# A two-layer product with nested sums: where the second layer's odd transfers land, and which engine makes four sums of W_out

## The chip, the cores and the metric

The kernel runs on one core of a Trainium2 chip. The metric is device time in microseconds (us) of one execution. The engines of the core are named as in the profile: PE (TensorE, matrix products), DVE (VectorE), ACT (ScalarE), POOL (GpSimd) and SP (SyncE, which here only issues DMAs). A line number such as L901 is a line of the kernel before.

## The reference

A masked attention on four batches of eight heads gives `x`, 3072 rows of 512 values. The change does not touch it. What follows is a feed-forward block:

```python
h = x @ w_in                                  # 3072x512 by 512x2048
g = h * (1.0 / (1.0 + np.exp(-1.702 * h)))
return (g @ w_out).astype(np.float32)         # 3072x2048 by 2048x512
```

All numbers are float32.

## The kernel before, in words

**Products by sums.** Both layers are computed with Winograd's form of Strassen's scheme: a product of 2x2 blocks takes seven products instead of eight, numbered 1 to 7 in the code, and needs four sums of quarters of each operand. `sums_a` (L219) makes those of the left operand (W): `s1 = a21 + a22`, `s3 = a11 - a21`, `s2 = s1 - a11`, `s4 = a12 - s2`. `sums_b` (L227) makes those of the right operand: `t1 = b12 - b11`, `d12 = b22 - b12`, `t2 = b22 - t1`, `t4 = b21 - t2`. In the profile a sum has the line of its formula: L222 to L225 for W, L230 to L233 for the other side. Products of the second layer are nested twice, so there are outer sums of W_out, inner sums of those, and inner sums of `g`.

**First layer.** 24 steps n = 8·sb + mt (`sb` is a block of 1024 rows, `mt` a strip of 128 hidden columns). The last two, 22 and 23, run outside the nested pairs, in the loop at L1391, each through `hidden` (L1083). Step 23 issues its products in the order 6, 5, 7, 2, 4, 3 (its product 1 belongs to step 22). Product 5 goes to PSUM bank `b`. At L1109 DVE adds that bank to `c22`. Product 3 (L1127) is accumulated onto the same bank `b`, so PE may start it only when the sum of L1109 has read the bank; the trace has this sum, and all sums of this helper, under L919. Products 5 and 6 read the sums of W_in, `s_in[:, 0:2]`. The results of a step are put to `g_dram` as seven blocks: three straight from `hidden`, four as POOL sums in `outer_sums` (L1140), which runs for step 22 before `hidden` of step 23 is emitted, and for step 23 at its end.

**Second layer.** 21 steps n (three blocks of rows, outer products in the order 1, 2, 6, 7, 5, 3, 4). In `product_of_halves` (L1228) each has seven products of 128x256 tiles, in PE's order 1, 2, 3, 6, 7, 5, 4, one after another without a gap if all operands are there. The block of `g` of step n comes by `fetch(n)` (L1186), two DMAs of 1 MB on SP's queue (one of 2 MB for the last step): even n into columns of `w_in_sb` (rows of 2 KB, four to a partition and DMA), odd n into `raw_g` (8 KB in one piece). DVE makes the inner sums of `g` (`g_sums`, L1206): product 5 needs t1 (L230), product 6 needs t2 (L232), product 7 needs d12 (L231, in place), product 4 needs t4 (L233). Those of step n+1 are made during step n, at the places called `after(0)` to `after(3)`. DVE also adds up the products (L1244).

**W_out.** Its outer sums are made in halves `c`, `low` and `high` (L1341), each a list of four sums s1, s3, s2, s4 of 128x1024 values: in `high`, DVE makes s1 and s2 (`high[0]`, `high[2]`), POOL makes s3 and s4 (`high[1]`, `high[3]`). The inner sums of W_out (`inner_sums(at)`, L1176) are POOL's, each of 128x512 values, kept in `rooms` (L1163), pieces of `xT`, of `w_in_sb` columns that are no longer needed, and of `s_in`. Outer product at = 2 of the order (n = 2) uses `inner_sums(2)`, and so on.

**Order.** The order on PE, DVE, ACT and POOL is that of the program text (`manual_schedule`); each engine runs its own list in order and waits where an operand is missing. SP's DMAs stand in one queue too. What L1391 to L1414 emits around step 23 is therefore the order of DVE: `high[0]`, t1 of n = 0 (`g[0]`), then in step 23 the sums to `c22` and `u`, t2 (`g[1]`, emitted "between"), the sum to `v`, then `high[2]`, d12 and t4. POOL's order there is: the inner sums of n = 1, the four outer sums of step 22, the four of step 23, `inner_sums(2)`, `high[1]`, `high[3]`.

Of the kernel before, what the change touches and what calls it, by code (L numbers as in the profile page):

```python
# [19 lines left out]
P = 128  # L20
# [18 lines left out]
def kernel(  # L39
# [806 lines left out]
    def feed_forward(tag, late=()):  # L846
# [9 lines left out]
        with ExitStack() as fctx:  # L856
# [283 lines left out]
            def outer_sums(*args):  # L1140
                last = args[0] * MT + args[1] == n1 * MT - 1
                t = [x.tile([P, XT], F32, tag=f"t{i}", name=f"t{i}") for x in places_of_sums for i in (1, 2, 4)]
                if last:
                    t = [s_in[:, 2, i // 2, i % 2 * XT : (i % 2 + 1) * XT] for i in range(3)]
                for i, (f, kept) in enumerate(g_outer(*args, *(t or (args[2], args[5], args[4])))):
                    f()

                    if last and i > 1:
                        kept_late.append(kept)
                    else:  # L1150
                        kept()

            places_of_sums, kept_late = [], []

            wqs = []

# [2 lines left out]
            flat = s_in.rearrange("p i k f -> p (i k f)")  # L1159
            rooms, s_rooms = ([x[:, i * F4 * P : (i + 1) * F4 * P].rearrange("p (c d) -> p c d", d=P) for i in range(count)]  # L1160
                              for x, count in ((xT[:, 3], 4), (flat, 12)))
            in_rooms = [w_in_sb[:, :, F2 * i + mt * P : F2 * i + (mt + 1) * P] for mt in range(4, FC // 2) for i in range(2)]
            rooms += in_rooms[:4] + s_rooms[:8] + in_rooms[4:] + s_rooms[8:]  # L1163
            wholes = [xT[:, i, 4 * XT : 6 * XT] for i in range(4)] + [t_x[:, i].rearrange("p k t -> p (k t)") for i in range(2)]
            wholes = [x.rearrange("p (q t) -> p q t", q=4) for x in wholes]

# [14 lines left out]
                return sums_a(nc.gpsimd, *w_quarters(OUTER[at])) if at < len(OUTER) else []  # L1181

            steps_out = [(sb, o) for sb in range(n1) for o in OUTER]
            raw_g = [w_in_sb.rearrange("p c (i f) -> p (c i) f", i=2)[:, :, 0:XT], None]

            def fetch(n):  # L1186
                sb, o = steps_out[n]
                parts = 1 if n + 1 == len(steps_out) else 2
                for h in range(parts):
                    cs = slice(h * FC // 2 // parts, (h + 1) * FC // 2 // parts)  # L1190
                    yield loader[0].dma_start(out=raw_g[n % 2][:, cs], in_=g_dram[len(LEFT) * sb + RIGHT[o], :, cs, :])

            g_tiles, wide = {}, []

            def g_quarters(n):
                if n not in g_tiles:


                    g_tiles[n] = wholes[4:6] if n == 1 else [
                        st2.tile([P, F4, TH], F32, tag=t, name=t + "b") for t in ("t1", "t2")] if n % 2 else wide[0:2]  # L1200
                    g_tiles[n] = g_tiles[n] + [wide[2]]
                g = raw_g[n % 2]
                x = [g[:, F4 * k : F4 * (k + 1), TH * j : TH * (j + 1)] for k in range(2) for j in range(2)]
                return x + g_tiles[n]

# [132 lines left out]
            for i in (list(range(1, LATE + 1)) if late else []) + free[:FC]:  # L1338
                todo[i] = [lambda: next(steps)] * 6

            low, high = ([sums_a(eng, *(x[:, :, F4 * c : F4 * (c + 1), :] for x in wqs))[i] for i, eng in enumerate(engs)]  # L1341
                         for c, engs in enumerate(((nc.gpsimd, nc.vector, nc.gpsimd, nc.gpsimd),
                                                   (nc.vector, nc.gpsimd, nc.vector, nc.gpsimd))))
            first = 2 * NESTED.stop
            todo[first] = high[:1] + inner_sums(1)

# [44 lines left out]
            for n in range(2 * NESTED.stop, 3 * MT):  # L1391
                sb, mt = divmod(n, MT)
                between, end = [], []
                if n == 2 * NESTED.stop:
                    whole(fetch(0))
                else:
                    assert not agenda
                    inner_ctx.close()
                    nest_ctx.close()
                    cv_ctx.close()  # L1400
                    sets[:] = [fctx.enter_context(tc.tile_pool(name=f"f{2 + i}{tag}", bufs=1, space=PSUM, side=side))
                               for i, side in enumerate(("right", "left"))]
                    gp = fctx.enter_context(tc.tile_pool(name=f"gp{tag}", bufs=1))
                    raw_g[1] = gp.tile([P, FC // 2, XT], F32, name="raw_g")
                    whole(fetch(1))
                    wide += [stage.tile([P, 4, TH], F32, tag=x, name="wide") for x in ("u", "v", "c21", "c22")]
                    t_ctx = fctx.enter_context(ExitStack())
                    places_of_sums.append(t_ctx.enter_context(tc.tile_pool(name=f"ts{tag}", bufs=1)))
                    g = g_sums(0)
                    g[0]()  # L1410
                    outer_sums(*heads.pop("sums"))
                    between, end = g[1:2], high[2:3] + g[2:] + inner_sums(2) + [high[1], high[3]]
                hidden(sb, mt, between, todo.pop(n, []) + end)
                yield  # L1414
            t_ctx.close()
# [5 lines left out]
            for n, (sb, o) in enumerate(steps_out):  # L1421
                final = n + 1 == len(steps_out)
                if 0 < n and n + 1 < len(steps_out):
                    dmas = list(fetch(n + 1))
                    while kept_late:
                        kept_late.pop(0)()
                        for dma in dmas:
                            behind_issue(stored[-1], dma)

                if n in (2, 3, 5, 6):  # L1430

                    nc.gpsimd.tensor_copy(mark, (g_quarters(n)[5] if n < 4 else ms[OUTER[n - 1]])[0:1, 0, 0:1])
                for f in {2: inner_sums(3), 3: inner_sums(4), 5: inner_sums(5) + inner_sums(6)[:2], 6: inner_sums(6)[2:]}.get(n, []):
                    f()
                later_sums = g_sums(n + 1)
                m = wholes[n % len(wholes)]

                def after(at, last=None):
                    if at == 0:
                        while pending:  # L1440
                            pending.pop(0)()
                    todo = [[x] for x in later_sums] if n == 0 else [[], later_sums[0:1], later_sums[1:3], later_sums[3:]]
                    todo = todo[at] if not final else []
                    if n + 2 >= len(steps_out):
                        turns = [lambda q=q: turned(m, int(final), int(not final), q, q + 1, last if q == 2 else None) for q in range(4)]
                        write = [lambda x=(sb, int(not final), (h,), loader + [nc.scalar] * (final or h == 0)): written(*x) for h in range(2)]
                        if final:
                            todo = [[], last_sum, [turns[1]], [turns[3], write[1]], [turns[0]], [turns[2], write[0]]][at]
                        elif at == 2:
                            todo = [later_sums[1], turns[1], turns[3], write[1]]  # L1450
                        elif at == 3:
                            todo = [turns[2], turns[0], later_sums[2]]
                            pending.append(write[0])
                            last_sum.append(later_sums[3])
                    for f in todo:
                        f()

                acc = {6: 1, 7: 6, 2: 1, 3: 6, 4: 7}.get(o)
                if o == 3:
                    pending.pop(0)()  # L1460
                ms[o] = product_of_halves(n, None if acc is None else ms[acc], after)

                def flat(x):
                    return x.rearrange("p q t -> p (q t)")

                if o == 5:
                    m5, m6, m7 = (ms[i] for i in (5, 6, 7))
                    pending += [lambda a=m6, b=m5: nc.vector.tensor_tensor(flat(a), flat(a), flat(b), op=Alu.add),
                                lambda a=m5, b=m7: nc.vector.tensor_tensor(flat(a), flat(a), flat(b), op=Alu.add),
                                lambda a=m5: turned(a, 1, 1, 0, 4)]  # L1470
                elif o in (2, 3) and n + 2 < len(steps_out):
                    pending.append(lambda a=ms[o], j=int(o == 3): turned(a, 0, j, 0, 4))
                    if o == 3:
                        pending.append(lambda sb=sb: written(sb, 1, (0, 1), loader))
                elif o == 4 and not final:
                    pending.append(lambda a=ms[4]: turned(a, 1, 0, 0, 4))
                    pending.append(lambda sb=sb: written(sb, 0, (0, 1), loader))
                yield

    def whole(steps):  # L1480
        for _ in steps:
            pass
# [49 lines left out]
```

## Time and profile before

| | us |
|---|---|
| median of 3 runs | 851.23 |
| lowest and highest | 850.65, 851.99 |
| the profiled execution | 850.31 |
| its span (first to last instruction) | 848.5 |
| PE busy | 837.3 |
| DVE busy | 679.2 |
| POOL busy | 376.9 |
| ACT busy | 337.6 |

The profiled execution's time lies 1.81 us above its span, and 0.92 us below the median of the runs. A row of a timeline has the start, the duration, the engine, the line, the operation, what it writes and reads, the shape, the count of merged instructions, and in brackets the idle time before it with what ended it. A duration counts from when the engine takes up the instruction, so an instruction that is held up shows as a long one.

### The profile page before, as it was taken

The numbers are of one execution on the slowest core, as the hardware profiler recorded it, in microseconds if no ns is written. First come the engines' busy times: TensorE is split into PE (matmuls) and PEld (weight loads), VectorE is DVE, ScalarE is ACT, GpSimd is POOL, SyncE is SP. The second block draws the span as 40 slices with busy tenths as digits, with TensorE's granted clock in tenths as the row PEclk, the third lists the DMA queues.
The fourth block names the chain that finished last, engine by engine and source line by source line (L and its number), as shares of the span: only waits on it lengthen the run. The fifth ranks groups of instructions, "written<-read, shape, count | busy, mean of one in ns | idle before, by whom it ended". The sixth has DMA issues, their size and how long they took to land.

```text
span 848.5 us, 14972 instructions
## 1 busy us (share of the span) xinstructions
PE 837.3 (99%) x5662; PEld 523.2 (62%) x5662; DVE 679.2 (80%) x1079; ACT 337.6 (40%) x550; POOL 376.9 (44%) x322
## 2 busy tenths in 40 slices
PE   9999999999999999999999999999999999999996
PEld 4444444444444444565666666656888888888885
DVE  5478888887888985778887888847899977797776
ACT  7766766767675634433444344442000000000000
POOL 5433443434343359996843487858865100000000
PEclk9999999999999999999999999999999999999999
DMA  8688667677663104455555545667844685468524
GB/s 145 120 156 170 156 131 146 144 150 151 151 154 95 48 2 173 149 173 213 211 203 195 197 181 216 237 232 249 298 153 168 198 270 193 157 202 248 195 102 101
DMA packets 173149, 144.92 MB, mean 171 GB/s; under 512 B 124112, under 2 KB 140112, under 8 KB 170512
## 3 DMA queue, kind: packets, MB, share of 16 engines
q1 hardware_dynamic: 162160, 110.54, 46.8%
q10 hardware_dynamic: 10912, 33.39, 11.9%
q8 instruction: 45, 0.74, 0.4%
q14 instruction: 32, 0.26, 0.1%
HBM read 79.69 MB, written 50.33 MB: 153 GB/s over the span
## 4 chain that ended last, share of the span: by engine, by line
PE 97%; DVE 2%; POOL 1%; issue 0%; POOLq 0%
PE product L1239 29%; PE product L901 22%; PE s L547 15%; PE s L514 15%; PE small L971 7%; PE product L971 4%; PE s L496 2%; PE s L460 1%; PE s L569 1%; DVE xT L1244 1%; DVE wide L232 0%; POOL above L339 0%; PE s L410 0%; POOL feat L337 0%; DVE wide L1244 0%
## 5 line engine op out<-in xcount | busy, mean ns | idle before, releaser
L484 ACT ACTIVATE e<-s 128x768 f32<-128x768 f32 x192 | 143.2, 811 | 48.8 <-PE s L514 43.9
L547 PE MATMUL s<-e,v 128*32 128x385 f32 x1536 | 130.9, 488 | 0.0
L525 POOL TENSOR_TENSOR t_x<-e 128x768 f32<-128x768 f32 x32 | 60.6, 1892 | 136.2 <-ACT e L484 131.3
L901 PE MATMUL product<-xT,w_in_sb 128*128 128x512 f32 x208 | 96.8, 592 | 0.0
L547 PEld LDWEIGHTS s<-e,v 128*32 128x32 f32 x1536 | 46.7, 109 | 79.3 <-issue 62.6
L901 PE MATMUL product<-t_x,s_in 128*128 128x512 f32 x192 | 89.8, 592 | 0.0
L514 PE MATMUL s<-s_in 32*128 32x384 f32 x912 | 87.8, 481 | 0.0
L525 POOL TENSOR_TENSOR t_x<-t_x,e 128x768 f32<-128x768 f32 x32 | 55.2, 1724 | 43.4 <-ACT e L484 42.0
L538 DVE TENSOR_TENSOR acc<-acc,e 128x768 f32<-128x768 f32 x63 | 70.1, 1112 | 2.3
L1275 ACT COPY wide<-product 128x256 f32<-128x256 f32 x20 | 7.4, 372 | 161.2 <-PE product L1239 127.9
L901 PEld LDWEIGHTS product<-xT,w_in_sb 128*128 128x128 f32 x208 | 39.4, 190 | 31.8 <-issue 28.9
L514 PEld LDWEIGHTS s<-s_in 32*128 32x128 f32 x912 | 43.9, 185 | 23.4 <-issue 2.2
L901 PEld LDWEIGHTS product<-t_x,s_in 128*128 128x128 f32 x192 | 36.4, 190 | 28.1 <-issue 24.9
L919 DVE TENSOR_TENSOR u<-product,u 128x256 f32<-128x256 f32 (+1 forms) x64 | 29.7, 477 | 18.9 <-PE product L971 16.6
L514 PE MATMUL s<-own 32*128 32x384 f32 x432 | 44.3, 482 | 0.0
L465 DVE TENSOR_SCALAR f<-s,above,weight 128x384 bf16<-128x384 f32 x15 | 10.2, 677 | 39.3 <-PE s L569 33.9
L230 POOL TENSOR_TENSOR u<-v,u 128x1024 f32<-128x1024 f32 (+1 forms) x12 | 26.2, 2184 | 20.9 <-ACT v L916 12.4
L1239 PE MATMUL product<-w_in_sb,xT 128*128 128x256 f32 x152 | 35.1, 379 | 0.0
L535 DVE SCALAR_TENSOR_TENSOR acc<-t_x,e 128x768 f32<-128x768 f32 x31 | 29.3, 946 | 6.4 <-POOL t_x L525 3.5
L919 DVE TENSOR_TENSOR c<-small,c 128x256 f32<-128x256 f32 (+1 forms) x60 | 26.8, 461 | 9.2 <-PE small L971 9.1
L919 DVE TENSOR_TENSOR v<-small,v 128x256 f32<-128x256 f32 (+1 forms) x60 | 27.0, 464 | 7.3 <-PE small L971 4.9
L1035 ACT COPY c<-product 128x512 f32<-128x512 f32 x20 | 11.7, 587 | 52.0 <-DVE v L919 50.1
(299 smaller groups left out, 1807.2 us busy)
## 6 DMA issues: line engine op xcount, KB each, us to landing
w_in_sb<-g_dram SPq DMA_DIRECT2D x20, 1024.0 KB, 5.6
raw_g<-g_dram SPq DMA_DIRECT2D x20, 1024.0 KB, 6.1
g_dram<-c ACTq DMA_DIRECT2D x20, 512.0 KB, 3.0
raw<-in_moe_w_out_dram ACTq DMA_DIRECT2D x16, 512.0 KB, 3.7
raw<-in_moe_w_in_dram ACTq DMA_DIRECT2D x15, 512.0 KB, 3.8
s_in<-own SPq DMA_DIRECT2D x36, 192.0 KB, 4.0
v<-in_v_dram SPq DMA_DIRECT2D x16, 384.0 KB, 4.2
g_dram<-u ACTq DMA_DIRECT2D x10, 512.0 KB, 2.9
```

Of the source, the lines that this page charges most:

```text
L230: return [lambda: eng.tensor_tensor(t1, b12, b11, op=Alu.subtract), lambda: eng.tensor_tensor(b12, b22, b12, op=Alu.subtract), lambda: eng ...
L484: nc.scalar.activation(es[c][:, kt, :, 0:HS], ps[:, :, 0:HS], Act.Exp, scale=1.0 / D**0.5)
L496: nc.tensor.matmul(ps[:, j, 0:HS], a[hs, keys], m[hs, cols], start=at == 0, stop=at == 1)
L514: nc.tensor.matmul(ps[i][:, j, 0:HS], a[r0 : r0 + 32, keys], m[r0 : r0 + 32, cols], start=at == 0, stop=at == 2)
L525: nc.gpsimd.tensor_tensor(low_sum, low_sum if i else e[:, 0], e[:, i + 1], op=Alu.add)
L535: nc.vector.scalar_tensor_tensor(acc, terms[0], T * TINY, terms[1], op0=Alu.add, op1=Alu.add)
L538: nc.vector.tensor_tensor(acc, acc, terms[i + 1], op=Alu.add)
L547: nc.tensor.matmul(av[D * j + d : D * j + d + 32, :], vt[:, j, row, d : d + 32], es[c][:, t, j, :], start=(t == 0), stop=(t == T - 1))
L901: nc.tensor.matmul(ps, wq[LEFT[i]][:, kc, :], xq[RIGHT[i]][:, kc, :], start=(start and kc == 0), stop=(kc == K2 - 1), skip_group_check=not ...
L919: nc.vector.tensor_tensor(dst, x, y, op=Alu.add)
L971: nc.tensor.matmul(x, wq[LEFT[i]], xq[RIGHT[i]], start=start, stop=True, skip_group_check=True)
L1239: nc.tensor.matmul(ps, wq[LEFT[i]][:, c, :], gq[RIGHT[i]][:, c, :], start=(onto is None and c == 0), stop=(c == F4 - 1), skip_group_check= ...
```

## The change

Five things are done:

1. `raw_g` gets a third place. `fetch(0)` still lands in `w_in_sb`; odd n still land in the pool tile; even n from 2 on (the third transfer, the fifth, and so on) land in the first 4096 values per partition of `s_in`, in one piece per partition.
2. `fetch(2)` is issued in the middle of step 23 (`between`), not at the head of step 1 of the second layer; the stores of the last two outer sums of step 23 are no longer put behind it (`kept_late` is gone).
3. `rooms` are laid out anew, so that the inner sums stay clear of `s_in[:, 0:2]`: sixteen pieces of `w_in_sb` columns and the last four of `s_in`.
4. `high[1]` and `high[3]` are made by DVE instead of POOL.
5. DVE's order around step 23 is now: `high[0]`, t1, **t2, `high[2]`**, then the sums to `c22` and `u`, **`high[1]`**, the sum to `v`, **`high[3]`**, d12, t4. POOL's list loses the two sums at its end; the rest of its order is as before.

```diff
-                for i, (f, kept) in enumerate(g_outer(*args, *(t or (args[2], args[5], args[4])))):
-                    f()
-
-                    if last and i > 1:
-                        kept_late.append(kept)
-                    else:
-                        kept()
+                for f in g_outer(*args, *(t or (args[2], args[5], args[4]))):
+                    for x in f:
+                        x()
...
-            in_rooms = [w_in_sb[:, :, F2 * i + mt * P : F2 * i + (mt + 1) * P] for mt in range(4, FC // 2) for i in range(2)]
-            rooms += in_rooms[:4] + s_rooms[:8] + in_rooms[4:] + s_rooms[8:]
+            in_rooms = [w_in_sb[:, :, F2 * i + mt * P : F2 * i + (mt + 1) * P] for mt in (4, 5, 6, 0, 1, 2, 3, 7) for i in range(2)]
+            rooms += in_rooms + s_rooms[8:]
...
-            raw_g = [w_in_sb.rearrange("p c (i f) -> p (c i) f", i=2)[:, :, 0:XT], None]
+            raw_g = [flat[:, 0 : 4 * F2].rearrange("p (c t) -> p c t", t=XT), None,
+                     w_in_sb.rearrange("p c (i f) -> p (c i) f", i=2)[:, :, 0:XT]]
+
+            def raw_of(n):
+                return raw_g[n % 2 if n else 2]
...
-                         for c, engs in enumerate(((nc.gpsimd, nc.vector, nc.gpsimd, nc.gpsimd),
-                                                   (nc.vector, nc.gpsimd, nc.vector, nc.gpsimd))))
+                         for c, engs in enumerate(((nc.gpsimd, nc.vector, nc.gpsimd, nc.gpsimd), (nc.vector,) * 4)))
...
                     g = g_sums(0)
-                    g[0]()
+                    for f in g[:2] + high[2:3]:
+                        f()
                     outer_sums(*heads.pop("sums"))
-                    between, end = g[1:2], high[2:3] + g[2:] + inner_sums(2) + [high[1], high[3]]
+                    between, end = [lambda: fetch(2), high[1]], high[3:] + g[2:] + inner_sums(2)
                 hidden(sb, mt, between, todo.pop(n, []) + end)
...
                 if 0 < n and n + 1 < len(steps_out):
-                    dmas = list(fetch(n + 1))
-                    while kept_late:
-                        kept_late.pop(0)()
-                        for dma in dmas:
-                            behind_issue(stored[-1], dma)
+                    if n > 1:
+                        fetch(n + 1)
```

More of the change, by code (lines that the diff above doesn't have):

```diff
@@ L1144, in outer_sums @@
                     t = [s_in[:, 2, i // 2, i % 2 * XT : (i % 2 + 1) * XT] for i in range(3)]
-                for i, (f, kept) in enumerate(g_outer(*args, *(t or (args[2], args[5], args[4])))):
-                    f()
-                    if last and i > 1:
-                        kept_late.append(kept)
-                    else:
-                        kept()
-            places_of_sums, kept_late = [], []
+                for f in g_outer(*args, *(t or (args[2], args[5], args[4]))):
+                    for x in f:
+                        x()
+            places_of_sums = []
             wqs = []
@@ L1190, in fetch @@
                     cs = slice(h * FC // 2 // parts, (h + 1) * FC // 2 // parts)
-                    yield loader[0].dma_start(out=raw_g[n % 2][:, cs], in_=g_dram[len(LEFT) * sb + RIGHT[o], :, cs, :])
+                    loader[0].dma_start(out=raw_of(n)[:, cs], in_=g_dram[len(LEFT) * sb + RIGHT[o], :, cs, :])
             g_tiles, wide = {}, []
@@ L1201, in g_quarters @@
                     g_tiles[n] = g_tiles[n] + [wide[2]]
-                g = raw_g[n % 2]
+                g = raw_of(n)
                 x = [g[:, F4 * k : F4 * (k + 1), TH * j : TH * (j + 1)] for k in range(2) for j in range(2)]
@@ L1394, in feed_forward @@
                 if n == 2 * NESTED.stop:
-                    whole(fetch(0))
+                    fetch(0)
                 else:
@@ L1404, in feed_forward @@
                     raw_g[1] = gp.tile([P, FC // 2, XT], F32, name="raw_g")
-                    whole(fetch(1))
+                    fetch(1)
                     wide += [stage.tile([P, 4, TH], F32, tag=x, name="wide") for x in ("u", "v", "c21", "c22")]
```

## The prediction

> **What bounds the kernel now.** I read the page's chain first, then PE's waits from 560 us on, where the change works.
>
> ```profile
> PE 97%; DVE 2%; POOL 1%; issue 0%; POOLq 0%
> PE product L1239 <- DVE wide L232: 2.5, 2, 2.2
> ```
>
> PE is the chain: 97% of it. So an edit counts only by what PE waits. From 560 us to the end it waits for one thing, twice, 2.5 us together: t2 of a second-layer step (DVE, L232). No wait of PE for a DMA is listed there. Timeline rows of PE (two products of step 0, three of step 2, where the longer wait is), then of DVE and POOL ahead of that wait:
>
> ```profile
> 591.60 1.89 PE L1239 MATMUL product<-w_in_sb,xT 128*128 128x256 f32 x8
> 595.05 1.89 PE L1239 MATMUL product<-wide,w_out_sb 128*128 128x256 f32 x8
> 612.32 1.89 PE L1239 MATMUL product<-w_in_sb,s_in 128*128 128x256 f32 x8
> 616.40 1.97 PE L1239 MATMUL product<-wide,s_in 128*128 128x256 f32 x8 [2.19 <-DVE wide L232]
> 618.20 1.89 PE L1239 MATMUL product<-w_in_sb,xT 128*128 128x256 f32 x8
> ...
> 606.86 3.98 DVE L1244 TENSOR_TENSOR xT<-xT 128x256 f32<-128x256 f32 x2
> 610.75 2.57 DVE L1244 TENSOR_TENSOR xT<-xT,wide 128x256 f32<-128x256 f32 x1
> 613.25 1.21 DVE L230 TENSOR_TENSOR wide<-w_in_sb 128x1024 f32<-128x1024 f32 x1
> 614.38 0.74 DVE L1244 TENSOR_TENSOR xT<-product,xT 128x256 f32<-128x256 f32 x2
> 615.05 1.21 DVE L232 TENSOR_TENSOR wide<-w_in_sb,wide 128x1024 f32<-128x1024 f32 x1
> ...
> 606.73 1.33 POOL L225 TENSOR_TENSOR s_in<-xT,s_in 128x512 f32<-128x512 f32 x1
> 608.02 2.53 POOL L223 TENSOR_TENSOR w_out_sb<-w_out_sb 128x1024 f32<-128x1024 f32 x1
> 610.51 2.54 POOL L225 TENSOR_TENSOR xT<-w_out_sb,xT 128x1024 f32<-128x1024 f32 x1
> ```
>
> Products start 1.73 us apart (products 7 and 4 of step 0, with one between them: 595.05 - 591.60 = 3.45), so product 6 of step 2 was due at 612.32 + 1.73 = 614.05. It starts at 616.40, 2.35 late, 0.14 after t2 ends (615.05 + 1.21 = 616.26); the next one follows after 1.80 instead of 1.73. Cost: **2.42**. Why DVE is late: three adds of 128x256, two of them in the row of 3.98 us, end just after POOL's sums do (610.84 after 610.55, 613.32 after 613.05). Those two POOL sums are `high[1]` and `high[3]`.
>
> **How the two engines take turns.** The rows of step 23, in order of time:
>
> ```profile
> 570.81 2.35 POOL L232 TENSOR_TENSOR c<-c,u 128x1024 f32<-128x1024 f32 x1
> 575.10 1.22 DVE L222 TENSOR_TENSOR xT<-w_out_sb 128x1024 f32<-128x1024 f32 x1
> 576.23 1.22 DVE L230 TENSOR_TENSOR wide<-w_in_sb 128x1024 f32<-128x1024 f32 x1
> 576.61 3.05 POOL L233 TENSOR_TENSOR s_in<-c,c 128x1024 f32<-128x1024 f32 x1 [3.44 <-ACT c L916]
> 579.61 1.27 POOL L222 TENSOR_TENSOR w_in_sb<-w_out_sb 128x512 f32<-128x512 f32 x1
> 580.36 0.69 DVE L919 TENSOR_TENSOR c<-product,c 128x512 f32<-128x512 f32 x1 [2.91 <-ACT c L1108]
> 582.97 1.88 PE L901 MATMUL product<-xT,s_in 128*128 128x512 f32 x4
> 585.50 1.37 DVE L224 TENSOR_TENSOR xT<-xT,w_out_sb 128x1024 f32<-128x1024 f32 x1
> 585.75 2.25 POOL L230 TENSOR_TENSOR t<-v,u 128x512 f32<-128x512 f32 x1
> 586.79 2.29 DVE L231 TENSOR_TENSOR w_in_sb<-w_in_sb 128x1024 f32<-128x1024 f32 x1
> 588.08 2.13 POOL L231 TENSOR_TENSOR v<-c,v 128x512 f32<-128x512 f32 x1
> ```
>
> Undisturbed, a sum takes 2.35 (POOL, 1024 values), 1.27 (POOL, 512), 1.22 (DVE, 1024); DVE's next starts 1.13 after. The row of 576.61 takes 3.05: it worked only from 579.66 - 2.35 = 577.31, which is 0.14 before DVE's sum ended (577.45). From 585.50 on each sum waits out exactly one of the other engine's and then goes. So a sum with both inputs in SBUF excludes the other engine's, a waiter begins 0.14 before the holder's recorded end, and they alternate. A DVE sum that reads a PSUM product isn't held up (0.69 at 580.36, while POOL's L222 works).
>
> The Trainium skill's "SBUF — State Buffer", section "Who interferes with whom", has the exclusion but says only that whoever issues first gets the port for its whole instruction; the turns are this trace's.
>
> **The change part by part.**
>
> *Removed: `high[1]`, `high[3]` on POOL.* From 608 us on, POOL has nothing of 2.5 us to put in DVE's way. After: 2.42 lower, if DVE's lateness from the new order is made up by then (below).
>
> *Added: t2 and `high[2]` ahead of the `c22` sum.* Here DVE was idle 2.91 us, but POOL's 1024-sum holds the port. Step by step: t2 is issued at 576.23 + 1.13 = 577.36; POOL is ahead until 579.66, so t2 works from 579.52 and ends at 580.74. POOL's L222 (issued 579.61) then works from 580.60 to 581.87. `high[2]` works from 581.73 to 582.95. The `c22` sum, until now at 580.36, starts 0.08 before that end, as DVE's next row does throughout (575.10 + 1.22 = 576.32, next 576.23), at 582.87, and ends at 583.56. Behind it wait the `u` sum, `high[1]`, and PE: product 3 of step 23 accumulates onto the bank that this sum reads. PE starts 0.14 after it, at 583.70 instead of 582.97: 0.73, and 0.08 for a start after a wait (1.80 against 1.73, 0.07 rounded up): **0.81** that the kernel does not have today. Bounds: nothing, if DVE goes first at 577.36 and POOL waits; 0.81 + 1.13 for each further POOL sum that gets in between (1.27 - 0.14). I take 0.81, since the rows alternate.
>
> *Added: `high[1]`, `high[3]` on DVE.* Each costs 1.13 and lets one POOL sum in. `high[1]` lies beside product 3, before the `v` sum; `high[3]` takes the place that `high[2]` leaves before d12. Alternating on: `high[1]` ends at 586.4, `v` at 587.0, `high[3]` at 588.6, d12 at 590.8, t4 at 593.0; today d12 ends at 589.08. DVE and POOL are both some 1.75 later. Products 7 and 4 of step 0 need d12 and t4: they start at 591.60 and 595.05 today, are due at 592.41 and 595.86 (0.81 later), 1.5 and 2.7 after their operands: no wait. Further on DVE waits for PE today:
>
> ```profile
> 603.88 0.42 DVE L1244 TENSOR_TENSOR wide<-product,wide 128x256 f32<-128x256 f32 x1 [0.93 <-PE product L1239]
> 605.61 0.42 DVE L1244 TENSOR_TENSOR xT<-product,wide 128x256 f32<-128x256 f32 x1 [1.30 <-PE product L1239]
> ```
>
> That is 2.23 of waiting; the lateness that counts, 1.75 - 0.81 = 0.94, goes there. Then, 0.81 after today: the add of 606.42, three SBUF adds, two of them behind POOL's last two inner sums of `inner_sums(2)` (today 606.73 is the last; it will end near 610.0), done by 610.5; t1 to 611.7; two product adds (0.74); t2 612.5 to 613.7. Product 6 is due at 614.05 + 0.81 = 614.86: 1.0 in hand after the 0.14. So the 2.42 is saved whole. Product 3 needs `inner_sums(2)` at 613.1, 3 after its end.
>
> *The second wait.*
>
> ```profile
> 663.14 1.89 PE L1239 MATMUL product<-w_in_sb,s_in 128*128 128x256 f32 x8
> 665.33 1.97 PE L1239 MATMUL product<-wide,s_in 128*128 128x256 f32 x8 [0.30 <-DVE wide L232]
> 643.01 1.25 POOL L222 TENSOR_TENSOR w_in_sb<-xT 128x512 f32<-128x512 f32 x1
> 644.34 1.27 POOL L223 TENSOR_TENSOR xT<-xT 128x512 f32<-128x512 f32 x1
> 644.69 1.20 DVE L1244 TENSOR_TENSOR t_x<-t_x,wide 128x256 f32<-128x256 f32 x1
> ```
>
> 665.33 - 664.87 + 0.07 = **0.53**. From 644.69 to there DVE never rests, so what it gains at 644.69 arrives. That add takes 1.20 instead of 0.42 behind POOL's second sum, whose series starts when DVE reaches a sum of step 4. DVE will be about 1 us less behind PE then, so POOL's series is earlier and most of the 0.78 goes; 0.46 is needed. I count 0.5 of it; bounds 0 and 0.53.
>
> *The transfers.*
>
> ```profile
> 579.68 0.37 SPq L911 DMA_DIRECT2D g_dram<-s_in  x1
> 595.79 0.39 SPq L911 DMA_DIRECT2D g_dram<-u  x1
> 598.70 1.06 SPq L1191 DMA_DIRECT2D w_in_sb<-g_dram  x2
> w_in_sb<-g_dram SPq DMA_DIRECT2D x20, 1024.0 KB, 5.6
> raw_g<-g_dram SPq DMA_DIRECT2D x20, 1024.0 KB, 6.1
> ```
>
> `fetch(2)` moves ahead of four stores, but still stands behind the store of `u`, which waits for POOL's sums of step 22, now 1.75 later: about 597.6, against 598.70. Its place is free by then (products 5 and 6 read it before 578; the store of 579.68 has 18 us to land). It lands near 604 and is wanted by product 1 of step 2, at 612.32 - 2 x 1.73 + 0.81 = 609.7. In one piece: `raw_g` is one piece already and takes 6.1 against 5.6, so no gain and no loss on PE. `fetch(3)` waits for the end of step 1's reading and is wanted 15 us later. The inner sums move from `s_in` to `w_in_sb` columns at the same duration (1.25 at 643.01 is such a one). All this: 0.
>
> **The sum.** -2.42 - 0.5 + 0.81 = -2.1. The profiled execution, 850.31, would become 848.2; it lies 0.92 below the median 851.23, so the median becomes **849.1**.
>
> **The rivals.**
>
> 1. *No new wait*: DVE keeps the port from 577.36 through t2 and `high[2]`, or POOL's sum comes later. -2.9, 848.3. For: DVE would be free. Against: POOL got in after one DVE sum at 576.61.
> 2. *One of the two old waits stays*: product 6 of step 2 has 1.0 in hand, the wait at 665 less. DVE's lateness carried on costs up to 1.3 of the gain, the 665 wait 0.5: -0.3 to -1.6, about 850.2.
> 3. *The same port time, only moved*: -2.42 fails to come since DVE makes two sums more. Then +0.81 stands alone, 852.0. Against: the port is held 2.5 by each sum on POOL, 1.1 on DVE. The Trainium skill's "Perfetto Trace Analysis", section "Optimizing Scalar/DVE Operations", warns that shifting work between these engines might not help, for the port they share; these rows speak for this direction.
> 4. *Slower*: PE's new wait outgrows the gain. Place: the `c22` sum. Price: 1.13 for each POOL sum beyond the two counted. It decides from 2.9, two further sums (0.81 + 2.26 = 3.07, 851.4); with four, all of POOL's inner sums and one of step 22's, 853.6 (-2.9 + 5.33 = +2.4). For: DVE's order is fixed, everything queues behind t2. Against: no row shows two POOL sums passing a waiting DVE sum.
> 5. *It doesn't do what it says*: the early transfer is early by 1 us and no one waits for it. That is already in the sum, as 0.
>
> **How the numbers follow.** Forecast (-1.5 to -2.7) 0.57; rival 1 0.12; rival 2 0.15; rival 3 0.06; rival 4, with any unseen stall, 0.10. About 0.2%, 1.7 us, is what a measurement tells from no change. The forecast's 2.1 is near it: 0.47 of its 0.57 are beyond. Faster 0.47 + 0.12 = 0.59; same 0.10 + 0.15 + 0.06 = 0.31; slower 0.10. Range: from rival 1 less the spread of the runs shown (848.3 - 0.6 = 847.7) up to rival 2's end and a bit of rival 4 (851.3).
>
> **What would show it.** Right: no wait of PE for L232; a new one of 0.7 for the `c22` sum (L919) before the last product of L901; a t2 row of 3.4 us at 577.4 and a `high[2]` row of 2.3. The steps fail if that wait is over 1.9 (POOL passed), absent (DVE kept the port), or if L232 still stands in PE's waits. A wait of PE or DVE for `s_in<-g_dram` would make the transfer part wrong.

## The result, and the profile after

| | before | after |
|---|---|---|
| median, us (runs) | 851.09 (8) | 848.69 (8) |
| lowest and highest, us | 850.17, 851.99 | 847.38, 849.15 |
| the profiled execution, us | 850.31 | 848.08 |
| its span, us | 848.5 | 846.3 |
| DVE busy, us | 679.2 | 682.2 |
| POOL busy, us | 376.9 | 372.6 |

The changed kernel takes 0.9969 of the time before, with a 95% interval from 0.9958 to 0.9979. The prediction was 849.1; the span fell by 2.2, where 2.1 were predicted. In the changed kernel L1239 of before has become L1240, and L1244 has become L1245.

First the same two views as for before, the page's chain and PE's waits from 560 us on.

```profile
PE 97%; DVE 1%; POOL 1%; issue 0%; POOLq 0%; DVEq 0%
PE product L901 <- DVE c L919: 0.5, 1, 0.5
```

PE is still the chain. Both waits for t2 (L232) are gone, and one for the sum to `c22` (L919) has come. PE's timeline shows the three places: the last products of step 23, then products 3 and 6 of step 2, then products 3, 6 and 7 of step 6.

```profile
581.21 1.88 PE L901 MATMUL product<-t_x,w_in_sb 128*128 128x512 f32 x4
583.55 1.98 PE L901 MATMUL product<-xT,s_in 128*128 128x512 f32 x4 [0.46 <-DVE c L919]
585.37 3.62 PE L1240 MATMUL product<-w_in_sb,w_out_sb 128*128 128x256 f32 x16
...
613.00 1.89 PE L1240 MATMUL product<-s_in,w_in_sb 128*128 128x256 f32 x8
614.73 1.89 PE L1240 MATMUL product<-wide,w_in_sb 128*128 128x256 f32 x8
...
661.35 1.89 PE L1240 MATMUL product<-s_in 128*128 128x256 f32 x8
663.07 1.96 PE L1240 MATMUL product<-wide,s_in 128*128 128x256 f32 x8
664.87 1.89 PE L1240 MATMUL product<-s_in,w_out_sb 128*128 128x256 f32 x8
```

How a wait's cost is read: product 3 of step 23 was due 1.72 after the one before it (in the trace of before these products start 1.71 to 1.72 apart), at 582.93, and started 0.62 later; the next one came 1.82 after it instead of 1.72. Together 0.72. The bracket says only 0.46, since it counts from the modelled end of the last matmul. In step 2 the products are 1.73 apart, without a wait. In step 6 product 6 also comes on time (663.07), with nothing in hand, as the rows of DVE will show; the one after it follows after 1.80 instead of 1.73, and this 0.07 is left out of the waits. So the sum is -2.42 - 0.53 + 0.72 = -2.2 (with the 0.07 as well), and that is the difference of the spans.

DVE's timeline, from t2 at 577 us to t2 of step 2, then POOL's:

```profile
577.43 3.25 DVE L232 TENSOR_TENSOR wide<-w_in_sb,wide 128x1024 f32<-128x1024 f32 x1
580.61 2.28 DVE L224 TENSOR_TENSOR xT<-xT,w_out_sb 128x1024 f32<-128x1024 f32 x1
582.82 0.68 DVE L919 TENSOR_TENSOR c<-product,c 128x512 f32<-128x512 f32 x1
...
590.69 2.29 DVE L233 TENSOR_TENSOR wide<-w_in_sb,wide 128x1024 f32<-128x1024 f32 x1
...
606.29 0.42 DVE L1245 TENSOR_TENSOR xT<-product,wide 128x256 f32<-128x256 f32 x1 [1.30 <-PE product L1240]
...
612.29 1.21 DVE L232 TENSOR_TENSOR wide<-s_in,wide 128x1024 f32<-128x1024 f32 x1
```

```profile
576.56 3.05 POOL L233 TENSOR_TENSOR s_in<-c,c 128x1024 f32<-128x1024 f32 x1 [3.14 <-ACT c L916]
579.56 2.25 POOL L222 TENSOR_TENSOR w_in_sb<-w_out_sb 128x512 f32<-128x512 f32 x1
...
608.62 1.33 POOL L225 TENSOR_TENSOR w_in_sb<-xT,w_in_sb 128x512 f32<-128x512 f32 x1
613.57 1.11 POOL L1430 COPY mark<-wide 1x1 f32<-1x1 f32 x1 [3.61 <-DVE wide L232]
```

t2 takes 3.25 because it waits out POOL's L233 (until 579.61) and then works for about 1.2; POOL's L222, 1.27 before, now takes 2.25 because it waits out t2; then DVE's L224 waits out that one. The engines alternate, sum by sum. At 608.62 POOL makes its last inner sum and has nothing more until 613.57: the two sums of 2.5 us that held DVE up in step 2 are not there, and t2 ends at 613.50, 1.2 before product 6 at 614.73.

### The profile page after: what moved, and what is told of

Same layout as the page of the kernel before. It is cut to its first block, busy times and chain, and to the rows that moved or that the text cites. A ratio compares the mean times of both kernels' runs of the same rounds, so it can differ in the third digit from the quotient of the medians.

```text
span 846.3 us, 14972 instructions
## 1 busy us (share of the span) xinstructions
PE 836.5 (99%) x5662; PEld 522.2 (62%) x5662; DVE 682.2 (81%) x1081; ACT 337.4 (40%) x550; POOL 372.6 (44%) x320
## 4 chain that ended last, share of the span: by engine, by line
PE 97%; DVE 1%; POOL 1%; issue 0%; POOLq 0%; DVEq 0%
PE product L1240 30%; PE product L901 21%; PE s L547 15%; PE s L514 15%; PE small L971 7%; PE product L971 4%; PE s L496 2%; PE s L460 1%; PE s L569 1%; DVE wide L232 0%; DVE xT L224 0%; POOL above L339 0%; PE s L410 0%; POOL feat L337 0%; DVE wide L230 0%
## 5 line engine op out<-in xcount | busy, mean ns | idle before, releaser
L919 DVE TENSOR_TENSOR u<-product,u 128x256 f32<-128x256 f32 (+1 forms) x64 | 29.7, 477 | 18.1 <-PE product L971 16.3
L919 DVE TENSOR_TENSOR c<-small,c 128x256 f32<-128x256 f32 (+1 forms) x60 | 26.8, 461 | 9.2 <-PE small L971 9.0
L919 DVE TENSOR_TENSOR v<-small,v 128x256 f32<-128x256 f32 (+1 forms) x60 | 27.1, 465 | 7.3 <-PE small L971 5.1
L1240 PE MATMUL product<-s_in,xT 128*128 128x256 f32 x136 | 31.3, 379 | 0.0
```

Of the source, the lines that this page charges most:

```text
L919: nc.vector.tensor_tensor(dst, x, y, op=Alu.add)
L1240: nc.tensor.matmul(ps, wq[LEFT[i]][:, c, :], gq[RIGHT[i]][:, c, :], start=(onto is None and c == 0), stop=(c == F4 - 1), skip_group_check= ...
```

## The experiments

Two accounts were to be told apart. The prediction's: the gain is the time for which POOL's two sums keep DVE out, and the price is one turn of POOL for each DVE sum ahead of the sum to `c22`. Against it: that the transfers bring the gain; that the whole 2.9 was to be had without a new wait, since DVE had time; and that the sums could have stayed where they were. All ratios are to the kernel before on the same chip, whose median is 851.26 for the first four rows, 851.15 for the next four and 851.47 for the last. A ratio comes with its interval from all the runs and is not the quotient of the two medians (for the engines only that would be 0.9982). "Waits" is the cost of PE's waits from 560 us on, worked out from PE's rows as above, without what a slower clock adds (last section); before it is 2.95.

| run | median, us | ratio, 95% interval | waits, us |
|---|---|---|---|
| transfers only | 851.42 | 1.0001 (0.9993 to 1.0010) | 2.98 |
| sums only | 848.41 | 0.9965 (0.9953 to 0.9977) | 0.72 |
| one sum ahead | 848.27 | 0.9965 (0.9953 to 0.9978) | 0.40 |
| three sums ahead | 851.89 | 1.0005 (0.9995 to 1.0015) | 2.8 |
| POOL in halves | 849.88 | 0.9989 (0.9980 to 0.9998) | 2.31 |
| engines only | 849.64 | 0.9991 (0.9982 to 1.0000) | 2.12 |
| behind t4 | 848.20 | 0.9966 (0.9955 to 0.9977) | 0.71 |
| the changed kernel again | 848.69 | 0.9972 (0.9963 to 0.9982) | 0.72 |
| four sums ahead | 854.78 | 1.0043 (1.0029 to 1.0056) | 5.0 |

### The transfers alone

The changed kernel with the engines and DVE's order of before:

```diff
-                    for f in g[:2] + high[2:3]:
-                        f()
+                    g[0]()
...
-                    between, end = [lambda: fetch(2), high[1]], high[3:] + g[2:] + inner_sums(2)
+                    between, end = [lambda: fetch(2), g[1]], high[2:3] + g[2:] + inner_sums(2) + [high[1], high[3]]
```

(`high` is again made by DVE, POOL, DVE, POOL.)

> The changed kernel's transfers, places of the inner sums and stores, with the sums of W_out and their order as before. Theory (the gain is two POOL sums taken out of DVE's way, less a new wait of PE): both waits of PE for t2 stay, 2.4 at step 2 and 0.5 at step 6, no wait for the c22 sum; 0 against before (within 0.4 us). Rival (the transfers bring the gain): 2.2 us faster than before, without the waits.

PE's waits from 560 us on:

```profile
PE product L1240 <- DVE wide L232: 2.5, 2, 2.2
```

This is the line of before: two waits for t2, the longer one 2.2. The ratio is 1.0001. Transfers in one piece, issued earlier and into another place, change nothing that can be measured here.

### The sums alone

The kernel before with parts 4 and 5 of the change and nothing else:

```diff
-                                                   (nc.vector, nc.gpsimd, nc.vector, nc.gpsimd))))
+                                                   (nc.vector,) * 4)))
...
-                    g[0]()
+                    for f in g[:2] + high[2:3]:
+                        f()
...
-                    between, end = g[1:2], high[2:3] + g[2:] + inner_sums(2) + [high[1], high[3]]
+                    between, end = high[1:2], high[3:] + g[2:] + inner_sums(2)
```

> The kernel before with only the sums changed: all four upper sums of W_out on DVE and DVE's new order; transfers, places and stores as before. Theory: no wait of PE for t2, one of 0.6 to 0.8 for the c22 sum; 2.2 us faster than before, as the changed kernel. Rival (transfers): 0 against before.

```profile
PE product L901 <- DVE c L919: 0.5, 1, 0.5
```

PE's waits are those of the changed kernel, and so is the ratio: 0.9965 against 0.9969, the intervals nearly the same. The four moved sums are the whole effect, gain and price.

### One sum ahead instead of two

The changed kernel, but `high[2]` goes behind the sums to `c22` and `u`; t2 alone stays ahead.

```diff
-                    for f in g[:2] + high[2:3]:
+                    for f in g[:2]:
...
-                    between, end = [lambda: fetch(2), high[1]], high[3:] + g[2:] + inner_sums(2)
+                    between, end = [lambda: fetch(2), high[2], high[1]], high[3:] + g[2:] + inner_sums(2)
```

> The changed kernel with only t2 ahead of the c22 sum, high[2] behind the u sum. t2 then ends near 580.7 and the c22 sum near 581.3, ahead of product 3 at 582.9. Theory A (waits add up): the new wait of 0.7 goes and nothing comes back, 2.9 us faster than before, 0.7 than the changed kernel. Theory B (DVE is the limit up to step 6; the new wait only gave it time): without it PE arrives 0.7 earlier at step 6, where t2 has about 0.25 in hand, and the old wait of 0.5 returns there; 2.4 to 2.5 faster than before, 0.2 to 0.3 than the changed kernel.

The sum to `c22` and t4 of step 5 on DVE, then PE's rows in step 6 (products 3, 6, 7):

```profile
581.07 0.68 DVE L919 TENSOR_TENSOR c<-product,c 128x512 f32<-128x512 f32 x1
...
650.57 1.95 DVE L233 TENSOR_TENSOR wide<-raw_g,t2b 128x1024 f32<-128x1024 f32 x1
```

```profile
661.08 1.89 PE L1240 MATMUL product<-s_in 128*128 128x256 f32 x8
663.13 1.97 PE L1240 MATMUL product<-wide,s_in 128*128 128x256 f32 x8 [0.17 <-DVE wide L232]
664.94 1.89 PE L1240 MATMUL product<-s_in,w_out_sb 128*128 128x256 f32 x8
```

The new wait is gone, but the old one of step 6 is back: product 6 was due at 661.08 + 1.73 = 662.81 and started at 663.13, and with the slow start after it that is 0.40. So removing a wait of 0.72 gained 0.32, the size that theory B gives. But DVE is not the limit all the way to step 6, as theory B has it: at 642.29 it still waits 1.30 for PE. What brings the wait back is t4 of step 5, which takes 1.95 here, behind a sum of POOL, and 1.21 in the changed kernel (the section after the experiments has the rows). In the time this can't be seen: 848.27 against 848.69, with intervals that overlap.

### Three sums ahead

The changed kernel with `high[1]` too ahead of the sum to `c22`:

```diff
-                    for f in g[:2] + high[2:3]:
+                    for f in g[:2] + high[2:3] + high[1:2]:
...
-                    between, end = [lambda: fetch(2), high[1]], high[3:] + g[2:] + inner_sums(2)
+                    between, end = [lambda: fetch(2)], high[3:] + g[2:] + inner_sums(2)
```

> The changed kernel with one sum more ahead of the c22 sum: t2, high[2] and high[1]. Theory (each such sum lets one POOL sum in, 1.08 + 1.13): the c22 sum ends 2.2 later, near 585.7, and PE waits 2.9 for it; no wait for t2 later; 0 against before (within 0.4). Rival (the order of DVE ahead of the c22 sum doesn't matter, DVE was idle there): as the changed kernel, 2.2 faster than before.

DVE's rows up to the sum to `c22`, and PE's around product 3:

```profile
580.30 2.28 DVE L224 TENSOR_TENSOR xT<-xT,w_out_sb 128x1024 f32<-128x1024 f32 x1
582.51 2.28 DVE L223 TENSOR_TENSOR w_out_sb<-w_out_sb 128x1024 f32<-128x1024 f32 x1
584.71 0.68 DVE L919 TENSOR_TENSOR c<-product,c 128x512 f32<-128x512 f32 x1
```

```profile
585.44 3.48 PE L901 MATMUL product<-xT,s_in 128*128 128x512 f32 x4 [2.66 <-DVE c L919]
588.76 3.62 PE L1240 MATMUL product<-w_in_sb,w_out_sb 128*128 128x256 f32 x16
```

Each sum ahead takes 2.2: 1.1 of its own and a turn of POOL. The `c22` sum comes at 584.71; it was at 581.07 with one and 582.82 with two sums ahead, but the traces don't start alike, so these are counted from the start of PE's product ahead of product 3 (581.67, 581.21 and 580.90): the sum lies 0.60 before it with one sum ahead, 1.61 behind it with two and 3.81 with three. Product 3, due at 580.90 + 1.72 = 582.62, is 2.8 late. The whole gain is spent. The place is that of the prediction's slower rival, but not the mechanism: there, further POOL sums were to pass one waiting DVE sum, and here each turn of POOL comes with a DVE sum of its own. The row of 3.48, instead of 1.98, is not explained by a wait; it comes up again below.

### POOL's two sums in halves

The kernel before, with `high[1]` and `high[3]` left to POOL at the same place, each as two sums of 512 values:

```diff
+                    halves = [sums_a(nc.gpsimd, *(x[:, i : i + 1, F4 : 2 * F4, :] for x in wqs)) for i in range(2)]
-                    between, end = g[1:2], high[2:3] + g[2:] + inner_sums(2) + [high[1], high[3]]
+                    between, end = g[1:2], high[2:3] + g[2:] + inner_sums(2) + [halves[i][k] for k in (1, 3) for i in range(2)]
```

> The kernel before, but POOL's high[1] and high[3] are each made as two sums of 512 values instead of one of 1024: the same work on the same engine at the same place, in twice as many turns. If what holds DVE up is the length of the one POOL sum that each add waits out (2.53 us), each of the three adds of 128x256 at 606.9 us now waits out about 1.27: DVE reaches t2 of step 2 some 1 to 2 us sooner, the wait of PE falls from 2.2 to between 0.4 and 1.5, and the wait in step 6 grows again, since DVE is the limit up to there: 0.6 to 1.1 us faster than before in all. If it is the sum of POOL's work that counts, or PE's wait had another cause, nothing changes: both waits stay as they are, 851.1.

DVE's rows ahead of t2 of step 2 (two adds, one add, t1), and products 3 and 6 on PE:

```profile
607.02 2.89 DVE L1244 TENSOR_TENSOR xT<-xT 128x256 f32<-128x256 f32 x2
609.84 1.49 DVE L1244 TENSOR_TENSOR xT<-xT,wide 128x256 f32<-128x256 f32 x1
611.25 2.29 DVE L230 TENSOR_TENSOR wide<-w_in_sb 128x1024 f32<-128x1024 f32 x1
```

```profile
612.48 1.89 PE L1239 MATMUL product<-w_in_sb,s_in 128*128 128x256 f32 x8
615.89 1.97 PE L1239 MATMUL product<-wide,s_in 128*128 128x256 f32 x8 [1.52 <-DVE wide L232]
```

The two rows that were 3.98 and 2.57 are 2.89 and 1.49: an add now waits out 1.3 instead of 2.5. But the last halves now stand in the way of t1 (2.29 instead of 1.21) and of t2 (1.62). The wait costs 1.75 instead of 2.42 (due at 612.48 + 1.73 = 614.21, started at 615.89, and a slow start after it); the one of step 6 stays, at 0.56. So what an add waits out is the single sum of POOL, not POOL's work as a whole; but halving the sums leaves 2.31 of waits, against 0.72 when they are gone from POOL. The wait in brackets, 1.52, is at the upper end of what was expected. The median fell by 1.27, twice the 0.64 of the waits; a part of that may be a slower clock in the kernel before (last section).

### The engines alone

The kernel before with `high[1]` and `high[3]` on DVE, straight behind `high[2]`; t2 and `high[2]` stay behind the sum to `c22`.

```diff
-                                                   (nc.vector, nc.gpsimd, nc.vector, nc.gpsimd))))
+                                                   (nc.vector,) * 4)))
...
-                    between, end = g[1:2], high[2:3] + g[2:] + inner_sums(2) + [high[1], high[3]]
+                    between, end = g[1:2], high[2:3] + [high[1], high[3]] + g[2:] + inner_sums(2)
```

> The kernel before with high[1] and high[3] on DVE, made straight behind high[2], and nothing else: t2 and high[2] stay where they were, after the sum to c22. The prediction's rules: no wait for the c22 sum any more (580.4 as before); high[1] and high[3] each cost DVE 1.13 and one POOL sum let in (1.13), so d12 ends 4.5 later, about 593.6, and product 7 of step 0, due at 591.6, waits 2.0 to 2.1 for it; no wait for t2 in steps 2 and 6 then, since PE is that much later. Sum: 2.1 + 0.1 of waits instead of 2.95 of before: about 0.8 faster than before and 1.4 slower than the changed kernel, 850.2. If two more DVE sums cost only their own 1.13 each, d12 ends 2.3 later, 591.4, no wait, and the gain is the whole 2.9 (848.2): then moving t2 and high[2] ahead of the c22 sum was a loss.

DVE's row of d12, and PE's last three products of step 0 (7, 5, 4):

```profile
591.38 2.28 DVE L231 TENSOR_TENSOR w_in_sb<-w_in_sb 128x1024 f32<-128x1024 f32 x1
```

```profile
593.80 3.49 PE L1239 MATMUL product<-w_in_sb,xT 128*128 128x256 f32 x8 [1.89 <-DVE w_in_sb L231]
597.08 2.10 PE L1239 MATMUL product<-wide,xT 128*128 128x256 f32 x8
599.02 1.89 PE L1239 MATMUL product<-wide,w_out_sb 128*128 128x256 f32 x8
```

d12 ends at 593.66, and product 7, due at 590.02 + 1.73 = 591.75, starts 2.05 late. No wait for the `c22` sum, none for t2. So each sum put on DVE does cost two turns here, and taking POOL's sums away is not enough by itself: nearly two thirds of the gain are lost if the two sums stand in front of what PE wants next. In place of 2.95 of waits there is a new one of 2.12; the ratio of 0.9991 is on the edge of what can be told from no change. (The profiled execution, with its row of 3.49, is one of the longer ones of this kernel, 851.4.)

### Behind t4

The same, but `high[1]` and `high[3]` stand behind d12 and t4:

```diff
-                    between, end = g[1:2], high[2:3] + g[2:] + inner_sums(2) + [high[1], high[3]]
+                    between, end = g[1:2], high[2:3] + g[2:] + [high[1], high[3]] + inner_sums(2)
```

> As the run with the engines alone, but high[1] and high[3] stand behind d12 and t4, which are wanted sooner. Now nothing of step 0 waits. DVE reaches the sums of step 1 some 4.5 later than before, so d12 of step 1 ends about 603.7, when product 7 of that step is due (603.7): a wait of 0 to 0.4. From the idle 2.2 us at 603 and 605 and the port time of the two POOL sums DVE makes up most of it until step 2: no wait for t2 there. The wait in step 6 stays at 0.3 to 0.6, since DVE is the limit up to there. Sum of waits about 1.0 instead of 2.95: 1.7 to 2.2 faster than before, 849.2, a little behind or equal to the changed kernel, without its new wait for c22. If DVE's lateness costs more (products not added up in time, PE waits for banks), a wait for L1244 is seen and the gain is under 1.

PE's rows in step 1, and product 6 of step 6:

```profile
602.05 1.89 PE L1239 MATMUL product<-t_x,w_in_sb 128*128 128x256 f32 x8
603.91 1.99 PE L1239 MATMUL product<-raw_g,w_out_sb 128*128 128x256 f32 x8
605.74 1.89 PE L1239 MATMUL product<-t_x,w_in_sb 128*128 128x256 f32 x8
...
663.13 1.97 PE L1239 MATMUL product<-wide,s_in 128*128 128x256 f32 x8 [0.25 <-DVE wide L232]
```

Product 7 of step 1 starts 0.13 late, behind d12, and the next one 0.10 more, too little for a line among the waits; product 6 of step 6, due at 660.99 + 1.73 = 662.72, costs 0.48 with the start after it. Together 0.71, as much as in the changed kernel, and the ratio agrees: 0.9966. So the move ahead of the sum to `c22` isn't needed: what matters is that POOL's two sums go, and that DVE makes them where nothing is due.

### The changed kernel again

No edit: the changed kernel beside the last three.

> The changed kernel once more, beside the others on one chip: 0.9969 of before (848.5 to 848.8), with one wait for the c22 sum of 0.4 to 0.6 in the list of PE's waits.

0.9972, and the one wait for the `c22` sum of 0.5. No version here beats the changed kernel by more than the intervals can tell; t2 alone ahead and `high[1]`, `high[3]` behind t4 come out 0.4 and 0.5 lower, and each of those waits for t2 in step 6 again (0.40 and 0.48).

### Four sums ahead

The changed kernel with t2 and all three of `high[2]`, `high[1]`, `high[3]` ahead of the `c22` sum:

```diff
-                    for f in g[:2] + high[2:3]:
+                    for f in g[:2] + high[2:3] + high[1:2] + high[3:]:
...
-                    between, end = [lambda: fetch(2), high[1]], high[3:] + g[2:] + inner_sums(2)
+                    between, end = [lambda: fetch(2)], g[2:] + inner_sums(2)
```

> The changed kernel with high[1] and high[3] also ahead of the sum to c22 (t2, high[2], high[1], high[3]). Two questions. First the price of a sum ahead: with t2 alone ahead the sum to c22 stands at 581.1, with two sums at 582.8, with three at 584.7; each sum of DVE with the POOL sum that it lets in costs 2.2, so the c22 sum comes at 586.9 and PE waits 4.9 to 5.1, for nothing else later. If DVE's sums went through without a turn for POOL, 1.1 more, the wait is 3.8. Second, the clock. In the profile with three sums ahead (wait 2.66) the product behind the wait took 3.48 instead of 1.98, at a granted clock of 0.57, and in that with the engines alone (wait 1.89) 3.49 instead of 1.97, at 0.56; in the profiles of before (2.19) and of the halves (1.52) it did not. The times of those kernels lie in two groups some 1.8 apart, those with waits up to 0.5 in one. If a long wait of PE by chance brings the half clock on, a wait of 5 brings it in every execution, and the times stand in one group: 850.6 (before without it) - 2.95 + 5.1 + 1.5 to 1.8 = 854.3 to 854.6. If the two groups have nothing to do with the wait, they remain, at 852.8 and 854.6. The Trainium skill, page TensorE: Matmul & The Clock Gate, Part 1, has the clock halved after an idle window of about 3.4 us; by that rule the waits of 1.9 and 2.7 should not have done it.

```profile
588.63 3.78 PE L901 MATMUL product<-xT,s_in 128*128 128x512 f32 x4 [4.86 <-DVE c L919]
592.21 4.69 PE L1240 MATMUL product<-w_in_sb,w_out_sb 128*128 128x256 f32 x16
596.74 1.89 PE L1240 MATMUL product<-w_in_sb,xT 128*128 128x256 f32 x8
```

Product 3 was due at 581.89 + 1.72 = 583.61 and is 5.02 late, 2.2 more than with three sums ahead (2.82). So each further sum ahead, from the second to the fourth, costs 2.2. The products behind the wait take 3.58 and 4.53 to the next start, instead of 1.72 and 3.45: another 2.9, which the last section is about. All five executions, 854.04 to 856.37, lie above the 852.8 that the wait alone would give. They don't stand in one group at 854.3 to 854.6 as was expected: two of them lie 1.5 and 1.8 above it.

## Why the prediction was right

- **"After: 2.42 lower".** Right. Product 6 of step 2 starts on time; t2 ends at 613.50, predicted 613.7. Shown from three sides: the sums alone bring the gain, the transfers alone don't, and with POOL's sums in halves the wait shrinks.
- **The new wait, 0.81.** Right in mechanism, 0.72 in size. The turns came as worked out, within 0.07: t2 577.43 to 580.68 (577.36 to 580.74 predicted), the `c22` sum 582.82 to 583.50 (582.87 to 583.56). What was mis-sized is PE's start after the sum: 0.05 instead of the 0.14 that was read from the waits for t2. Rival 1, no new wait, is out.
- **"DVE and POOL are both some 1.75 later", with no wait in step 0.** Right: t4, 590.69 + 2.29, ends at 592.98, predicted 593.0. Of the 2.23 that DVE waited for PE at 603 to 606 us, the row of 606.29 is left with 1.30; the 0.93 that went is the predicted 0.94.
- **The second wait, -0.5.** Right in size, wrong in its place. It was put down to the add that took 1.20 behind POOL's second sum. POOL's series did come earlier, as predicted: its first sum starts 2.65 ahead of that add (640.25 to 642.90) instead of 1.68 (643.01 to 644.69). But the add takes longer now, 1.46. The gain came later, at t4 of step 5, which a sum of POOL (L223) no longer held up. The rows of after, then those of before:

```profile
642.90 1.46 DVE L1245 TENSOR_TENSOR t_x<-t_x,wide 128x256 f32<-128x256 f32 x1
647.77 2.13 POOL L223 TENSOR_TENSOR w_out_sb<-w_out_sb 128x512 f32<-128x512 f32 x1
651.24 1.21 DVE L233 TENSOR_TENSOR wide<-raw_g,t2b 128x1024 f32<-128x1024 f32 x1
...
661.71 1.22 DVE L232 TENSOR_TENSOR wide<-s_in,wide 128x1024 f32<-128x1024 f32 x1
```

```profile
651.52 2.13 POOL L223 TENSOR_TENSOR w_out_sb<-w_out_sb 128x512 f32<-128x512 f32 x1
652.78 1.95 DVE L233 TENSOR_TENSOR wide<-raw_g,t2b 128x1024 f32<-128x1024 f32 x1
```

From the add to t2 of step 6 DVE needs 18.81 (642.90 to 661.71) where it needed 19.28 (644.69 to 663.97, by t2's end 0.14 ahead of product 6 at 665.33). t2 ends at 662.93, 0.14 ahead of product 6 at 663.07: nothing in hand. That the 0.47 gained just covers the 0.46 needed is luck. With one sum ahead POOL's series starts only 1.83 ahead of the add (640.80 to 642.63), t4 is held up again (1.95), and from the add to t2 DVE needs 19.14: so only 0.32 of the 0.72 came. Of the eleven traces, the five with a wait in step 6 have t4 at 1.95 or 1.96, the six without have it at 1.21. The prediction had no such step: its rival 1 counts the whole 2.9 as to be had, and 2.55 (2.95 - 0.40) came.

- **The transfers, 0.** Right, and shown by the run with them alone (1.0001). `fetch(2)` was issued at 597.98, predicted 597.6.
- **Rival 2, an old wait stays.** Not in this kernel. But one sum ahead and behind t4 each have the wait of step 6 still, so it was near.
- **Rival 3, port time only moved.** Out. The Trainium skill, page "Perfetto Trace Analysis", section "Optimizing Scalar/DVE Operations", warns that moving work between DVE and POOL might not help. For the engines alone, with the sums put in front of d12, the run agrees (0.9991); put behind t4, the same two sums bring the whole gain (0.9966). Here the place on DVE's list decides.
- **Rival 4, slower at the `c22` sum.** Not this kernel, and its mechanism was not seen: no trace shows two POOL sums passing a waiting DVE sum. A wait at that place does grow with more DVE sums ahead: 2.8 with one more, 5.0 with two, the latter 0.43% slower than before (0.29% to 0.56%), with the slower clock in it.
- **The time.** 849.1 against 848.69. Of the 0.4, 0.1 lies in the profiled execution (848.08 instead of 848.2), which is the waits. The other 0.3 is its distance from the median, which was carried over from before (0.92) and is 0.61 after. The prediction gave no reason why it should carry over; in the eight runs of before it is 0.78.

## What to carry to other kernels

When two engines exclude each other, look at the place as well as at the length: a sum costs its own time and one turn of the other engine to whatever stands behind it in the queue, so put it where the next consumer has that much in hand. Before counting the removal of a wait as gain, follow the slower engine on to its next wait: here 0.72 off PE was worth 0.32, since some 70 us later a sum of DVE had to wait out a sum of POOL again. And count a PE wait of about 2 us as more than its length (next section).

## What the runs showed of the hardware that was not expected

**A PE wait of about 2 us can halve PE's clock afterwards.** The busy times by stretch for three runs: the granted clock is the third number from the end. The lines are the stretches behind the wait with three sums ahead, then with the engines alone, then with four sums ahead.

```profile
585.40:589.00 3.60, 3.56 (x6) 1.73 (x7) 0.63 (x2) 1.71 (x3) 3.44 (x4) 0.57 0.58 241
```

```profile
593.80:597.10 3.30, 3.30 (x9) 2.64 (x10) 3.30 (x3) 0.00 (x0) 3.22 (x3) 0.54 0.40 145
597.10:599.00 1.90, 1.90 (x9) 1.65 (x8) 1.79 (x4) 0.00 (x0) 1.90 (x1) 0.90 0.97 358
```

```profile
587.60:591.50 3.90, 2.87 (x4) 1.32 (x5) 1.58 (x3) 1.71 (x3) 3.82 (x3) 0.50 0.21 85
591.50:597.00 5.50, 5.50 (x20) 4.22 (x19) 4.54 (x3) 1.00 (x2) 5.34 (x5) 0.74 0.67 249
```

With the engines alone the clock lacks 0.46 x 3.30 + 0.10 x 1.90 = 1.7 us, 3.4 us at half speed; PE's rows say the same, (597.08 - 593.80 - 1.80) + (599.02 - 597.08 - 1.73) = 1.7. With four sums ahead it lacks 0.50 x 3.90 + 0.26 x 5.50 = 3.4, twice as much. In the profiled execution of before the clock stays at 1.00 behind the wait of 2.19, and likewise with the halves (1.52). It doesn't happen in every execution: of the executions of kernels whose longest wait is 1.9 to 2.7 us, many have a mean clock of 0.996 or less (before 31 of 60, transfers only 8 of 12, three sums ahead 5 of 12, engines only 3 of 11); of the 48 of kernels with no wait over 1.6 us, none has. That the low mean comes from this wait in each of them was not shown, since one execution of a kernel has a trace (two of the changed kernel). The mean is a rough sign, too: in every trace the clock also falls to half at the end, behind PE's last product (in before it is 0.50 from 847 us on), and with that alone the mean is 0.997 to 0.999. The executions with the low mean are 1.7 and 1.6 longer on average with three sums ahead and the engines alone, but only 1.0 and 1.1 for before and the transfers alone; why less there was not shown. The Trainium skill, page "TensorE: Matmul & The Clock Gate", Part 1, gives the step to half clock and a window of about 3.4 us, which agree with the 1.7 us lost, one or two times; but it asks for a whole idle window, and here waits of 1.89 and 2.66 were enough. If that clock is what makes half of the executions of before 1.0 longer, it adds some 0.5 to their mean, and this is why times fell by more than waits here (2.40 against 2.2 for the change); that was argued, not shown.

**PE starts at different distances after DVE.** 0.05 after a sum that read its PSUM bank (583.50 to 583.55), 0.14 after a sum that makes its operand (with one sum ahead, 661.77 + 1.22 = 662.99 to 663.13). The prediction took the second for both. It is no rule by the kind of sum: with the sums behind t4, product 7 of step 1 starts 0.05 after the d12 that is its operand (602.24 + 1.62 = 603.86 to 603.91). What decides was not shown.
